# Attention kernel on one core: products with V on 64-row tiles in two banks, in two pieces a step

## The chip, the cores and the metric

The kernel runs on one core of one Trainium2 chip. The metric is device time in microseconds (us) of one execution. TensorE is PE in the profile (its weight loads PEld), VectorE is DVE, ScalarE is ACT, GpSimd is POOL, SyncE (which issues the DMAs) is SP.

## What is computed

A transformer block of 2048 tokens and width 512, all in float32: attention with 32 heads of 16 that share one key and one value head, then a gated feed-forward part of width 1792. Both are preceded by a layer norm that a vector c modulates.

```
mod = (silu(c) @ w_mod)          # sa, ca, ga, sb, cb, gb
h = layernorm(x) * (1 + ca) + sa
q = h @ wq  (32 heads of 16);  k = h @ wk;  v = h @ wv      # one k, one v
p = softmax(q k^T / 4);  o = p v
x = x + ga * (o @ wo)
h = layernorm(x) * (1 + cb) + sb
x = x + gb * ((sigmoid(h @ w_gate) * (h @ w_up)) @ w_down)
```

## The kernel before

**Units and steps.** The queries are cut into 4 blocks of 512 (b), the heads into 8 groups of four (u). A unit i is one (b, u); there are 32. Each unit has 16 steps, one for each 128 keys (kb), so there are 512 steps, s = 16 i + kb. After them comes a tail with the feed-forward part of the last block.

**A step.** `scores(n)` for n = 0 to 3 makes one tile of transposed scores `st` (128 keys x 512 queries, for one head; `st_tile`) and one tile `sa` of scores the other way round (128 queries x 512 keys; `a_tile`), which belongs to a later unit. ACT turns each `st` into exponentials `P`. DVE takes the row maxima of each `sa` (`mx`). The maxima go into spare rows of the queries `qp`, so that `st` comes out with the maximum already taken off. Queries and keys are split into high and low 16-bit halves that lie in one contraction of 64 rows, which is why `st` and `sa` have 64 rows: one takes the upper 64 rows of the array, the other the lower 64, and the two run at once.

**Products with V** (`pv`): for each of the four heads of the unit, V (128 keys x 32 columns, 16 of them ones, which give the softmax's sums) is the stationary operand and P the moving one, in float32. Head hh writes partitions 32 hh to 32 hh + 31 of one PSUM bank `c`, so a product takes 128 rows and 32 columns of the array, and four run at once. They lag the scores by LAG = 2 steps (`vq`). In a step with feed-forward work (`full`) all 512 queries are done in one piece, after `scores(1)`. In other steps they are done in two halves of 256, after `scores(1)` and after `scores(3)`. In unit 0 the order of keys and queries differs (`parts`), and a tile holds four pieces of 128 queries.

**The end of a unit** (`unit_end`): DVE copies `c` to `cs`; DMAs take the sums to DRAM (`lD`) and the rows to `raw`; some steps later (W1, W2, W3) the reciprocals come back and POOL multiplies.

**Maxima**: after the 64th `sa` tile of a unit, `max_end` reduces on DVE at the next step's start, and `max_rows` transposes the result on PE into a bank of the `sa` pool. ACT copies it out (`m`), POOL splits it, and DMAs put it into `qp`.

**Feed-forward work** of block b - 1 (and, in block 0, the remaining products for q) is laid between the scores of block b. A `Couple` holds two accumulation groups of 64-row products, so that two products run at once, each on one half of the array. `plan(s)` starts a couple, decides over how many steps it goes (RATE = 4.5 pairs a step) and lists the sizes of its places (`places`); `piece()` runs the next place. There are three places a step: after `scores(0)`, after `scores(2)` and after `scores(3)`. In the middle of a couple the two groups change halves, and one place there is left empty. The transposes of the normalised rows (`tr`, four for each group) go in two places of two. In block 0 `light(s)` places the q products after `scores(0)`.

**Order.** From the first step on, the order on PE, DVE and ACT is the order of the code (`keep`, by way of `Ordered`; hence line 116 for nearly all of it).

**PSUM** has 8 banks: `c` 1, `st` 2, `sa` 3, and 2 for everything else (`bank`).

Of the kernel before, what the change touches and what calls it, by code (L numbers as in the profile page):

```python
# [10 lines left out]
AF = mybir.ActivationFunctionType  # L11
ALU = mybir.AluOpType
# [10 lines left out]
QB = 512  # L23
NB = S // QB
NKB = S // P
NDC = D // P
NFC = F // P
NU = 8
# [14 lines left out]
LAG = 2  # L43
# [7 lines left out]
RATE = 4.5  # L51
# [6 lines left out]
W3 = 2  # L58

PBUFS = 4  # L60
SBANKS = {"st": 2, "sa": 3}
GWB = 3
HBUFS = 36

# [2 lines left out]
def adaln_mqa_glu_kernel(  # L67
# [15 lines left out]
    pool, sp = nc.gpsimd, nc.sync  # L83
# [16 lines left out]
    def bank(name):  # L100
        return psum["b"].tile([P, 512], F32, tag="b", name=name, bufs=psum.get("n", 7))

    def sbank(name):
        return psum["s"].tile([P, 512], F32, tag=name, name=name, bufs=SBANKS[name]) if "s" in psum else bank(name)

    def cbank(name):
        return pc.tile([P, 512], F32, tag="c", name=name, bufs=1)
# [10 lines left out]
    pinned = []  # L118
    pe, dve, act = Ordered(nc.tensor), Ordered(nc.vector), Ordered(nc.scalar)
# [45 lines left out]
    def t32(name, shape=(P, 512)):  # L165
        return wp.tile(list(shape), F32, tag="f32", name=name, bufs=18)
# [156 lines left out]
    V = cp.tile([P, NKB, 32], F32, name="V")  # L323
# [93 lines left out]
    Cs = {}  # L417
    Ps = {}
# [71 lines left out]
    def parts(i, t):  # L490
        if i == 0:
            return [(4 * (t % 4) + n, slice(n * P, (n + 1) * P), slice(t // 4 * P, (t // 4 + 1) * P)) for n in range(4)]
        return [(t, slice(0, QB), slice(0, QB))]
# [12 lines left out]

    def pv(i, t, half=None):
        if t == 0 and half != 1:  # L510
            Cs[i] = cbank("c")
        ps = parts(i, t)
        if half is not None:
            if i == 0:
                ps = ps[2 * half:2 * half + 2]
            else:
                cut = slice(half * QB // 2, (half + 1) * QB // 2)
                ps = [(t, cut, cut)]
        for kb, cols, qs in ps:
            for hh in range(4):  # L520
                pe.matmul(Cs[i][32 * hh:32 * hh + 32, qs], V[:, kb, :], Ps[i, t, hh][:, cols],
                          start=(kb == 0 and (i == 0 or half != 1)), stop=(kb == NKB - 1 and (i == 0 or half != 0)))
        if half == 0:
            return
        for hh in range(4):
            del Ps[i, t, hh]
        if t == NKB - 1:
            unit_end(i)

    def unit_end(i):  # L530
        b, u = units[i]
        o, v = u // 2, u % 2
        cs = t32("cs")
        if pinned:
            dve.tensor_copy(cs, Cs.pop(i))
        else:
            act.activation(cs, Cs.pop(i), AF.Identity)
        if v == 0:
            raws[b, o] = t32("raw")
        raw = raws[b, o]  # L540
        half = slice(4 * DH * v, 4 * DH * (v + 1))

        def rows(dst, r0):
            for hh in range(4):
                g = 4 * v + hh
                sp.dma_start(dst[DH * g:DH * (g + 1)], cs[32 * hh + r0:32 * hh + r0 + DH])

        if u >= NU - 2 and b == NB - 1:

            if v == 0:  # L550
                rbs[b, o] = t32("rb")
            rb = rbs[b, o]
            rows(rb, DH)
            rows(raw, 0)
            dve.reciprocal(rb[half], rb[half])
            if v == 0:
                return
        else:
            if v == 0:
                rbs[b, o] = dr.tile([2, 8, QB], F32, tag="lD", name="lD", bufs=2)  # L560
            lD = rbs[b, o]
            sp.dma_start(lD[0, 4 * v:4 * v + 4], cs[DH:P:2 * DH])
            rows(raw, 0)
            if v == 0:
                return
            defer(W1, lambda: recip(b, o, lD, raw))
            return
        finish(b, o, raw, rb, u == NU - 1 and b == NB - 1)

    def recip(b, o, lD, raw):  # L570
        lc = wp.tile([P, 32], F32, tag="lc", name="lc", bufs=2)
        rc = wp.tile([P, 32], F32, tag="rc", name="rc", bufs=2)
        sp.dma_start(lc, lD[0].rearrange("h (s e) -> (h s) e", e=32))
        defer(W2, lambda: recip2(b, o, lD, raw, lc, rc))
# [23 lines left out]
    def defer(n, f_):  # L598
        waits.append((now[0] + n, f_))
# [35 lines left out]
    class Transposes:  # L635
        stage, n = "tr", 4
# [196 lines left out]
    psum["s"] = psum["ctx"].enter_context(tc.tile_pool(name="pa", bufs=1, space=PSUM, reuse_waits="tile"))  # L833
    psum["b"], psum["n"] = psum["s"], 7 - sum(SBANKS.values())
    pinned.append(True)
# [16 lines left out]
    run = []  # L852
    lead = [0.0]
# [1 line left out]


    def places(m, n):
        skip = 3 * (n - n // 2) - 1
        res = [3 if k + 1 == skip else (1, 2, 1)[k % 3] for k in range(3 * n)]
        for ks in (range(skip), range(skip + 1, 3 * n)):  # L860
            order = sorted(ks, key=lambda k: ((0, 2, 1)[k % 3], k))
            while sum(res[k] for k in ks) != m:
                d = 1 if sum(res[k] for k in ks) < m else -1
                res[order[0]] += d
                order.append(order.pop(0))
        res[skip] = 0
        return res

    def pick(s):
        while main and main[0][0] is None:  # L870
# [15 lines left out]

    def plan(s):
        if s < NU * NKB:
            return None
        if not run:  # L890
            g = pick(s)
            if g is None:
                lead[0] = 0.0
                return None
            if g.stage == "tr":
                n, sizes = 1, [2, 0, 2]
            else:
                least = -(-g.n // MOST)
                n = min(max(least, round((g.n + lead[0]) / RATE)), len(units) * NKB - s)
                if n < least:  # L900
                    spare.insert(0, g)
                    return None
                sizes = places(g.n // 2, n)
            at = 0
            for k, z in enumerate(sizes):
                run.append((g, at, at + z, n if k == 0 else 0))
                at += z
        lead[0] += sum(z[2] - z[1] for z in run[:3]) - RATE
        return "run"

    def piece():
        if run:
            g, n0, n1, _ = run.pop(0)
            if n1 > n0:
                g.part(n0, n1)

# [5 lines left out]
            early[c_].part(ats[n], ats[n + 1])  # L922

    vq = []
    before = None

    for i, (b, u) in enumerate(units):
        if u == 0 and b > 0:
            wos, trs, gs = ffn_groups(b - 1)
            gs = [Couple(*wos[:2]), Couple(*wos[2:])] + trs + gs  # L930
            main.extend([(b - 1, g) for g in gs[:-KEPT]] + [(None, None)] + [(b - 1, g) for g in gs[-KEPT:]])
        for kb in range(NKB):
            s = i * NKB + kb
            now[0] = s
            late, pend[:] = pend[:], []
            for z in [z for z in waits if z[0] <= s]:
                waits.remove(z)
                z[1]()
            rows = [max_end(*z) for z in late]
            an = A0 + 4 * s  # L940

            def scores(n):
                st_tile(i, kb, n // 2, n % 2)
                if an + (n ^ 1) < len(alist):
                    a_tile(*alist[an + (n ^ 1)])

            scores(0)
            if before == "run":
                piece()
            elif b == 0:  # L950
                light(s)
            scores(1)
            now_ = plan(s)
            full = now_ is not None
            if len(vq) >= LAG:
                pv(*vq[0], None if full else 0)
            for z in rows:
                z()
            scores(2)
            if now_ == "run":  # L960
                piece()
            scores(3)
            if len(vq) >= LAG:
                if not full:
                    pv(*vq[0], 1)
                vq.pop(0)
            if now_ == "run":
                piece()
            before = now_
            vq.append((i, kb))  # L970
            while wdone < nw:
                if wdone < nw - 4 and (wdone + 0.5) * WSTEPS > (s + 1) * (nw - 4):
                    break
                if wdone >= nw - 4 and s < WLAST + 3 * (wdone - nw + 4):
                    break
                wjobs[wdone]()
                wdone += 1
# [1 line left out]
    while run:  # L979
        piece()  # L980
    while vq:
        pv(*vq.pop(0))
    assert not waits
    psum["ctx"].close()
    psum["ctx"] = ctx.enter_context(ExitStack())
# [44 lines left out]
```

## Time and profile before

| | |
|---|---|
| median of 3 runs | 1741.75 us (1739.81 to 1743.01) |
| span of the profiled execution | 1738.4 us |
| what lies around the span, to the median | 3.35 us |
| PE busy | 1691.9 us, 97% of the span |
| DVE busy | 1443.2 us, 83% |
| ACT busy | 1226.3 us, 71% |
| POOL busy | 605.1 us, 35% |
| mean granted TensorE clock | 0.983 |
| unit 0 (16 steps) | 115.4 to 158.6 us |
| units 1 to 7 (112 steps) | 158.6 to 451.3 us |
| tail | from 1592 us |

The page gives no time of the profiled execution apart from its span. A row of a group reads: line, engine, operation, written tile <- read tiles, shape, count | busy us, mean ns of one | idle us of the engine before them, and what ended it. For a matmul the shape begins with rows * columns of the array that it takes (64*128). A row of the timeline reads: start us, length us, engine, line, operation, tiles, shape, how many were merged. Matmuls are pipelined, so a record is longer than what it adds to the stream; starts tell more than lengths.

### The profile page before, as it was taken

The numbers are of one execution on the slowest core, as the hardware profiler recorded it, in microseconds if no ns is written. First come the engines' busy times: TensorE is split into PE (matmuls) and PEld (weight loads), VectorE is DVE, ScalarE is ACT, GpSimd is POOL, SyncE is SP. The second block draws the span as 40 slices with busy tenths as digits, with TensorE's granted clock in tenths as the row PEclk, the third lists the DMA queues.
The fourth block names the chain that finished last, engine by engine and source line by source line (L and its number), as shares of the span: only waits on it lengthen the run. The fifth ranks groups of instructions, "written<-read, shape, count | busy, mean of one in ns | idle before, by whom it ended". The sixth has DMA issues, their size and how long they took to land.

```text
span 1738.4 us, 35892 instructions
## 1 busy us (share of the span) xinstructions
PE 1691.9 (97%) x14467; PEld 591.1 (34%) x14467; DVE 1443.2 (83%) x2407; ACT 1226.3 (71%) x2231; POOL 605.1 (35%) x715
## 2 busy tenths in 40 slices
PE   5889999999999999999999999999999999999998
PEld 3335333333233333333333333333333333333443
DVE  8889999999998988888899898988898888841311
ACT  3338888888878777777778777777778777774100
POOL 4131445454443332332245232233255141231433
PEclk9769999999999999999999999999999999999999
DMA  7111223231100110111111110011101010011211
GB/s 262 40 47 31 95 85 106 89 110 63 51 23 26 47 49 12 33 38 41 32 41 33 33 50 20 26 47 47 36 17 57 28 57 5 30 50 55 75 60 49
DMA packets 66238, 90.94 MB, mean 52 GB/s; under 512 B 14752, under 2 KB 41376, under 8 KB 66072
## 3 DMA queue, kind: packets, MB, share of 16 engines
q1 hardware_dynamic: 66072, 88.66, 15.6%
q8 instruction: 113, 1.85, 0.4%
q14 instruction: 53, 0.43, 0.1%
HBM read 67.68 MB, written 16.22 MB: 48 GB/s over the span
## 4 chain that ended last, share of the span: by engine, by line
PE 86%; DVE 7%; ACT 2%; POOL 1%; issue 1%; DMA 1%; SPq 0%; POOLq 0%; DVEq 0%; ACTq 0%
PE c L116 27%; PE st L116 20%; PE pgu L116 12%; PE sa L116 8%; PE pd L116 5%; PE pgu L139 4%; DVE mx L116 3%; PE pd L139 2%; PE pq L116 2%; PE po L116 2%; ACT P L116 2%; PE sa L451 1%; DVE mx L453 1%; PE pmod L222 1%; PE pt L116 1%
## 5 line engine op out<-in xcount | busy, mean ns | idle before, releaser
L116 ACT ACTIVATE P<-st 128x512 f32<-128x512 f32 x2048 | 1139.2, 595 | 283.7 <-PE sa L116 250.0
L116 DVE TENSOR_REDUCE mx<-sa 128x1 f32<-128x512 f32 x1972 | 1241.2, 684 | 113.6 <-PE sa L116 108.3
L116 PE MATMUL st<-qp,kp 64*128 64x512 f16 (+1 forms) x2240 | 746.8, 362 | 7.1 <-DVE mx L453 2.4
L116 PE MATMUL sa<-kp,qp 64*128 64x512 f16 x1972 | 725.3, 382 | 0.5 <-DVE mx L116 0.5
L116 PE MATMUL c<-P,V 128*32 128x512 f32 (+2 forms) x5552 | 577.6, 492 | 2.9 <-DVE cs L116 2.9
L116 PEld LDWEIGHTS <-kp 64*128 64x128 f16 x2240 | 187.8, 94 | 500.1 <-issue 407.2
L116 PE MATMUL pgu<-h2h,gw 64*128 64x512 f16 x1344 | 242.6, 376 | 0.0
L116 PEld LDWEIGHTS <-qp 64*128 64x128 f16 x1972 | 181.8, 93 | 137.0 <-issue 51.9
L116 PEld LDWEIGHTS c<-P,V 128*32 128x32 f32 x5552 | 111.5, 108 | 192.1 <-issue 177.3
L727 POOL TENSOR_SCALAR th<-th 128x512 f32<-128x512 f32 x42 | 26.0, 619 | 335.8 <-ACT th L116 325.8
L116 PE MATMUL pgu<-h2l,gw 64*128 64x512 f16 x672 | 132.3, 376 | 0.0
L116 PEld LDWEIGHTS <-gw 64*128 64x128 f16 x2016 | 99.6, 94 | 80.7 <-issue 3.1
L424 POOL MEMSET qp<- 32x2048 f16 x32 | 57.6, 1798 | 49.3 <-PE st L116 41.6
L139 PE MATMUL pgu<-h2h,gw 128*128 128x512 f16 x224 | 66.8, 379 | 0.5 <-ACT h2h L283 0.5
L733 POOL TENSOR_TENSOR gl<-th,gh 128x512 f16<-128x512 f32 x56 | 64.8, 1157 | 4.7
L478 POOL TENSOR_SCALAR mh<-m 16x128 f16<-16x128 f32 (+1 forms) x34 | 9.8, 288 | 159.3 <-ACT m L116 159.0
L730 DVE SCALAR_TENSOR_TENSOR th<-th,pgu 128x512 f32<-128x512 f32 x14 | 9.6, 688 | 66.3 <-PE pgu L139 53.0
L248 POOL TENSOR_SCALAR wst<-wst 128x512 f32<-128x512 f32 x46 | 28.5, 620 | 102.1 <-DMA wst<-in_B_w_down_dram 27.1
L721 ACT ACTIVATE th<-pgu 128x512 f32<-128x512 f32 x14 | 8.4, 597 | 76.9 <-PE pgu L139 76.9
L116 DVE COPY u<-pgu 128x512 f32<-128x512 f32 x42 | 28.5, 679 | 35.7 <-PE st L116 19.8
L750 POOL TENSOR_TENSOR ot<-ot,gb 128x512 f32<-128x512 f32 x10 | 12.7, 1273 | 126.7 <-ACT ot L116 126.7
L590 POOL TENSOR_TENSOR raw<-raw,rb 128x512 f32<-128x512 f32 x15 | 19.1, 1273 | 102.7 <-DMA rb<-lD 84.1
(164 smaller groups left out, 1435.3 us busy)
## 6 DMA issues: line engine op xcount, KB each, us to landing
gw<-wD SPq DMA_DIRECT2D x56, 512.0 KB
wD<-gw SPq DMA_DIRECT2D x14, 512.0 KB
wm<-in_w_mod_dram SPq DMA_DIRECT2D x6, 1024.0 KB
qp<-qD SPq DMA_DIRECT2D x96, 64.0 KB
xall<-in_A_x_dram SPq DMA_DIRECT2D x4, 1024.0 KB
qD<-q SPq DMA_DIRECT2D x16, 256.0 KB
raw<-cs SPq DMA_DIRECT2D x128, 32.0 KB
xr<-in_A_x_dram SPq DMA_DIRECT2D x16, 256.0 KB
```

What stands on the lines that cost most here:

```text
L116: return (lambda *a, **k: keep(f_(*a, **k))) if pinned else f_
L139: pe.matmul(self.bank, l_, r_, start=(n == 0), stop=(n == self.n - 1))
L222: pe.matmul(p_[32 * k:32 * (k + 1)], cbc[:, k, :], wmods[i][:, k, :], start=True, stop=True)
L248: pool.tensor_scalar(w_, w_, SW, 0.0, op0=ALU.mult, op1=ALU.add)
L424: pool.memset(qp[j:j + 32], 0.0)
L451: pe.matmul(sa, qp[64 * j:64 * j + 64, pr0 + pr, qt * P:(qt + 1) * P], kp[64 * j:64 * j + 64, kc * 512:(kc + 1) * 512], start=True, stop=True)
L453: dve.tensor_reduce(mxs[i][:, 2 * j + pr, qt, kc:kc + 1], sa, axis=AX.X, op=ALU.max)
L478: pool.tensor_scalar(mh[:, 0], m32, 1.0, 0.0, op0=ALU.mult, op1=ALU.add)
L590: keep(pool.tensor_tensor(raw, raw, rb, op=ALU.mult))
L727: pool.tensor_scalar(th, th, 1.0, 1.0, op0=ALU.add, op1=ALU.mult)
L733: pool.tensor_tensor(lo, th, hi, op=ALU.subtract)
L750: pool.tensor_tensor(ot, ot, mods2['gb'], op=ALU.mult)
```

## The change

- **Products with V.** The contraction of 128 keys is cut into two of 64 (r = 0, 1). Each takes 64 rows and 32 columns of the array, so there are eight tiles. Row half 0 writes to bank `c`, row half 1 to a second bank `c1`. At a unit's end ACT copies the one bank, DVE the other, and POOL adds them (in the last unit DVE adds straight from PSUM).
- **Two pieces a step, always**: halves of 256 queries, normally after `scores(0)` and its feed-forward place, and after the third place. In the first step of a unit's products both are one turn later (`values`).
- **Banks.** `c1` takes one; `sa` has two instead of three.
- **Feed-forward work in four places a step**, one after each of the four scores; in the middle of a couple two places are empty. The transposes go in one place of four. `light(s)` and the maxima's transposes (`rows`) move one turn later.

```
-SBANKS = {"st": 2, "sa": 3}
+SBANKS = {"st": 2, "sa": 2, "c1": 1}
...
-    def pv(i, t, half=None):
-        if t == 0 and half != 1:
-            Cs[i] = cbank("c")
+    def pv(i, t, half):
+        if t == 0 and half == 0:
+            Cs[i] = (cbank("c"), sbank("c1"))
...
         for kb, cols, qs in ps:
-            for hh in range(4):
-                pe.matmul(Cs[i][32 * hh:32 * hh + 32, qs], V[:, kb, :], Ps[i, t, hh][:, cols],
-                          start=(kb == 0 and (i == 0 or half != 1)), stop=(kb == NKB - 1 and (i == 0 or half != 0)))
+            for r in range(2):
+                rs = slice(64 * r, 64 * r + 64)
+                for hh in range(4):
+                    pe.matmul(Cs[i][r][32 * hh:32 * hh + 32, qs], V[rs, kb, :], Ps[i, t, hh][rs, cols],
+                              start=(kb == 0 and (i == 0 or half == 0)),
+                              stop=(kb == NKB - 1 and (i == 0 or half == 1)))
...
-        cs = t32("cs")
-        if pinned:
-            dve.tensor_copy(cs, Cs.pop(i))
+        cs, cs1 = t32("cs"), t32("cs1")
+        c0, c1 = Cs.pop(i)
+        act.activation(cs, c0, AF.Identity)
+        if b == NB - 1 and u == NU - 1:
+            dve.tensor_tensor(cs, c1, cs, op=ALU.add)
         else:
-            act.activation(cs, Cs.pop(i), AF.Identity)
+            dve.tensor_copy(cs1, c1)
+            pool.tensor_tensor(cs, cs, cs1, op=ALU.add)
...
     def places(m, n):
...
+        k = 2 * n - 1
+        half = [m * (z + 1) // k - m * z // k for z in range(k)]
+        return half + [0, 0] + half
...
-                n, sizes = 1, [2, 0, 2]
+                n, sizes = 1, [0, 4, 0, 0]
...
+            plan(s)
+            vs = [(*vq[0], 0), (*vq[0], 1)] if len(vq) >= LAG else []
+            if vs and vs[0][1] == 0:
+                vs.insert(0, None)
+
+            def values():
+                if vs:
+                    z = vs.pop(0)
+                    if z is not None:
+                        pv(*z)
+
             scores(0)
-            if before == "run":
-                piece()
-            elif b == 0:
+            piece()
+            values()
+            scores(1)
+            if b == 0:
                 light(s)
-            scores(1)
-            now_ = plan(s)
-            full = now_ is not None
-            if len(vq) >= LAG:
-                pv(*vq[0], None if full else 0)
+            piece()
+            scores(2)
             for z in rows:
                 z()
-            scores(2)
-            if now_ == "run":
-                piece()
+            piece()
+            values()
             scores(3)
+            piece()
+            values()
             if len(vq) >= LAG:
-                if not full:
-                    pv(*vq[0], 1)
                 vq.pop(0)
-            if now_ == "run":
-                piece()
...
```

More of the change, by code (lines that the diff above doesn't have):

```diff
@@ L505, in st_tile @@
         Ps[i, t, 2 * pr + j] = p_[:, j]
-    def pv(i, t, half=None):
-        if t == 0 and half != 1:
-            Cs[i] = cbank("c")
+    def pv(i, t, half):
+        if t == 0 and half == 0:
+            Cs[i] = (cbank("c"), sbank("c1"))
         ps = parts(i, t)
[L513 to L518, printed above, removed]
-        for kb, cols, qs in ps:
-            for hh in range(4):
-                pe.matmul(Cs[i][32 * hh:32 * hh + 32, qs], V[:, kb, :], Ps[i, t, hh][:, cols],
-                          start=(kb == 0 and (i == 0 or half != 1)), stop=(kb == NKB - 1 and (i == 0 or half != 0)))
+        if i == 0:
+            ps = ps[2 * half:2 * half + 2]
+        else:
+            cut = slice(half * QB // 2, (half + 1) * QB // 2)
+            ps = [(t, cut, cut)]
+        for kb, cols, qs in ps:
+            for r in range(2):
[4 more added lines that the diff above has]
+                              stop=(kb == NKB - 1 and (i == 0 or half == 1)))
         if half == 0:
@@ L857, in places @@
     def places(m, n):
[L858 to L867, printed above, removed]
+        k = 2 * n - 1
+        half = [m * (z + 1) // k - m * z // k for z in range(k)]
+        return half + [0, 0] + half
     def pick(s):
@@ L888, in plan @@
         if s < NU * NKB:
-            return None
+            return
         if not run:
@@ L893, in plan @@
                 lead[0] = 0.0
-                return None
+                return
             if g.stage == "tr":
-                n, sizes = 1, [2, 0, 2]
+                n, sizes = 1, [0, 4, 0, 0]
             else:
@@ L901, in plan @@
                     spare.insert(0, g)
-                    return None
+                    return
                 sizes = places(g.n // 2, n)
             at = 0
-            for k, z in enumerate(sizes):
-                run.append((g, at, at + z, n if k == 0 else 0))
+            for z in sizes:
+                run.append((g, at, at + z))
                 at += z
-        lead[0] += sum(z[2] - z[1] for z in run[:3]) - RATE
-        return "run"
+        lead[0] += sum(z[2] - z[1] for z in run[:4]) - RATE
     def piece():
         if run:
-            g, n0, n1, _ = run.pop(0)
+            g, n0, n1 = run.pop(0)
             if n1 > n0:
@@ L924, in adaln_mqa_glu_kernel @@
     vq = []
-    before = None
     for i, (b, u) in enumerate(units):
@@ L945, in scores @@
                     a_tile(*alist[an + (n ^ 1)])
+            plan(s)
[7 more added lines that the diff above has]
+                        pv(*z)
             scores(0)
-            if before == "run":
-                piece()
-            elif b == 0:
+            piece()
+            values()
+            scores(1)
+            if b == 0:
                 light(s)
-            scores(1)
-            now_ = plan(s)
-            full = now_ is not None
-            if len(vq) >= LAG:
-                pv(*vq[0], None if full else 0)
+            piece()
+            scores(2)
             for z in rows:
                 z()
-            scores(2)
-            if now_ == "run":
-                piece()
+            piece()
+            values()
             scores(3)
+            piece()
+            values()
             if len(vq) >= LAG:
-                if not full:
-                    pv(*vq[0], 1)
                 vq.pop(0)
-            if now_ == "run":
-                piece()
-            before = now_
             vq.append((i, kb))
@@ L981, in adaln_mqa_glu_kernel @@
     while vq:
-        pv(*vq.pop(0))
+        for half in range(2):
+            pv(*vq[0], half)
+        vq.pop(0)
     assert not waits
```

## The prediction

> **What bounds the kernel now.** I read the page first, then busy time by stretch, the groups with shapes kept apart, and the timeline of single steps.
>
> ```profile
> span 1738.4 us, 35892 instructions
> PE 1691.9 (97%) x14467; PEld 591.1 (34%) x14467; DVE 1443.2 (83%) x2407; ACT 1226.3 (71%) x2231; POOL 605.1 (35%) x715
> PE 86%; DVE 7%; ACT 2%; POOL 1%; issue 1%; DMA 1%; SPq 0%; POOLq 0%; DVEq 0%; ACTq 0%
> ```
>
> PE carries 86% of the chain that ended last. A busy PE may still be slow inside, so I go by stretch (columns: PE, PEld, DVE, ACT, POOL busy us; clock; DMA).
>
> ```profile
> 158.60:451.30 292.70, 288.28 (x3032) 91.97 (x3028) 285.65 (x474) 252.97 (x463) 138.81 (x172) 1.00 0.27 87
> 540.80:1497.60 956.80, 955.86 (x7990) 315.84 (x7988) 859.43 (x1397) 744.64 (x1359) 306.10 (x347) 1.00 0.11 36
> ```
>
> The first row is units 1 to 7 of block 0 (112 steps): 292.7/112 = 2.61 us a step, PE and DVE both full. The second is 20 units with feed-forward work (320 steps): 2.99 us a step, PE at 99.9%, DVE at 90%. The granted clock is 1.00, so nothing comes from there.
>
> ```profile
> L116 PE MATMUL c<-P,V 128*32 128x512 f32 x2896 | 385.5, 604 | 0.0
> L116 PE MATMUL c<-P,V 128*32 128x256 f32 x2144 | 171.3, 391 | 2.9 <-DVE cs L116 2.9
> L116 PE MATMUL c<-P,V 128*32 128x128 f32 x512 | 21.1, 283 | 0.0
> ```
>
> Each product with V is two matmul records (two passes). A step with all 512 columns in one piece has 4 x 2 = 8 records: 2896/8 = 362 "whole" steps. A step in two halves has 16: 2144/16 = 134 "halved" steps. Unit 0 has 512/32 = 16. That is all 512 steps.
>
> **One whole step, one halved step.**
>
> ```profile
> 801.24 0.38 PE L116 MATMUL pgu<-h2h,gw 64*128 64x512 f16 x2
> 801.49 0.37 PE L116 MATMUL st<-qp,kp 64*128 64x512 f16 x1
> 801.50 0.39 PE L116 MATMUL sa<-kp,qp 64*128 64x512 f16 x1
> 801.82 1.06 PE L116 MATMUL c<-P,V 128*32 128x512 f32 x8
> 802.81 0.39 PE L116 MATMUL st<-qp,kp 64*128 64x512 f16 x1
> 802.82 0.39 PE L116 MATMUL sa<-kp,qp 64*128 64x512 f16 x1
> 803.04 0.38 PE L116 MATMUL pgu<-h2h,gw 64*128 64x512 f16 x2
> 803.26 0.38 PE L116 MATMUL sa<-kp,qp 64*128 64x512 f16 x1
> ...
> 351.08 0.64 PE L116 MATMUL c<-P,V 128*32 128x256 f32 x8
> 351.65 0.39 PE L116 MATMUL st<-qp,kp 64*128 64x512 f16 x1
> ```
>
> Two matmuls of 64 rows run side by side, one on each half of the array, and such a pair advances PE by 0.215 us (803.04 to 803.26). A piece of c lasts 0.99 us from its start to the next st for 512 columns (801.82 to 802.81) and 0.57 us for 256 (351.08 to 351.65). So 256 columns stream in 0.42 us, and 0.15 us of each piece does not depend on its width. Ahead of it, sa starts at 801.50, streams 0.215 us, and c starts 0.32 us after it: another 0.10 us. A piece therefore pays 0.25 us beyond its streaming, and PE's step adds up: 4 pairs of scores 0.86, feed-forward 4.5 pairs (RATE) 0.97, c 0.84 + 0.25 = 1.09; 2.92 of the 2.99 us.
>
> Is it the change of tile shape (the a*b in the rows) that costs the 0.25 us?
>
> ```profile
> 1591.63 0.61 PE L116 MATMUL c<-P,V 128*32 128x512 f32 x4
> 1592.17 0.39 PE L139 MATMUL po<-woh,ah 128*128 128x512 f16 x1
> ...
> 1620.46 0.38 PE L139 MATMUL pd<-wdh,gl 128*128 128x512 f16 x1
> 1620.67 0.49 PE L698 MATMUL pt<-ident,t 128*128 128x128 f32 x3
> ...
> 802.27 0.61 PE L116 MATMUL c<-P,V 128*32 128x512 f32 x4
> 802.29 0.59 PE L116 MATMUL c<-P,V 128*32 128x512 f32 x1
> ```
>
> At 1620.67 the type changes from f16 to f32 in one shape: 0.215 us after pd, no cost. At 1592.17 only the columns of the shape change (128*32 to 128*128, rows the same): the last second pass starts 0.02 us after the first of the four (802.27 and 802.29), so 1591.65 to 1592.17 is 0.52 us for 0.42 us of streaming, 0.10 us too long. That is just what c pays on its way to 64*128 (802.29 to 802.81, 0.52 us). A change of columns alone costs as much as a change of rows and columns.
>
> The Trainium skill ("TensorEngine Tiling (Array Packing)", section Key Properties) says that changing the tiling mode, and not just the tile, drains the TensorE, and its list of configurations has 64x128 and 64x32 as two modes. By that rule each new piece pays on entry and exit; the trace agrees where it can be seen, and no run here yet shows the two 64-row shapes side by side.
>
> **The change, part by part** (the sum is made against the span, 1738.4 us; the median of the runs, 1741.75, is 3.35 above it, and I add that at the end).
>
> (1) *Two pieces in every step.* The 362 whole steps pay for a second entry and exit: 362 x 0.25 = +90.5. If 64*32 beside 64*128 cost nothing, this would be a gain (rival B). I take the full 0.25 by the 1592.17 row, the nearest: a change of columns with equal rows. PE has no idle time there to hide it (955.86 of 956.80).
>
> (2) *Eight tiles instead of four.* The streaming stays 0.42 us per 256 columns if both halves of the array run together, as the st/sa pair does. Tiles start some 7 ns apart (0.02 us for three), so four more end the piece 0.027 us later: x 2 x 362 = +19.5; bounds 0 and twice that (39). The skill's "TensorE: Matmul & The Clock Gate" (Measured speedup vs the span model) has about 4 ns a tile, which would make this 11.6.
>
> (3) *Two banks for sa.* When does a bank come free?
>
> ```profile
> 1264.53 2.45 DVE L116 TENSOR_REDUCE mx<-sa 128x1 f32<-128x512 f32 x4
> 1265.24 0.37 PE L116 MATMUL sa<-kp,qp 64*128 64x512 f16 x1
> 805.70 0.39 PE L116 MATMUL sa<-kp,qp 64*128 64x512 f16 x1
> 806.15 2.48 DVE L116 TENSOR_REDUCE mx<-sa 128x1 f32<-128x512 f32 x4 [0.29 <-PE sa L116]
> PEld sa L116 <- DVE mx L116: 19.4, 25, 0.8
> L116 DVE TENSOR_REDUCE mx<-sa 128x1 f32<-128x512 f32 x1972 | 1241.2, 684 | 113.6 <-PE sa L116 108.3
> L116 DVE COPY u<-pgu 128x512 f32<-128x512 f32 x42 | 28.5, 679 | 35.7 <-PE st L116 19.8
> L116 DVE COPY cs<-c 128x512 f32<-128x512 f32 x32 | 22.0, 687 | 11.1 <-PE c L116 9.9
> L116 PE MATMUL sa<-ident,m 128*16 128x128 f32 x31 | 8.6, 277 | 0.5 <-DVE m L116 0.5
> ```
>
> A reduce starts 0.45 us after its matmul (805.70 to 806.15); reduces in a row come every 0.60 us ((2.45 - 0.68)/3, rounded); a waiting sa starts 0.71 us after its bank's reduce did (1264.53 to 1265.24). With three banks such waits sum to 19.4 us. With two, sa number k+2 waits for the start of reduce k plus 0.71, and st and all else on PE queue behind it. By hand:
> - Whole step, new order (pair 0.215, feed-forward 0.24 a place, piece 0.42 + 0.25 + 0.027 = 0.70): sa at 0, 1.155, 1.61, 2.77, next at 3.22; reduces start at 0.45, 1.60, 2.20, 3.22. The banks are wanted at 1.61, 2.77, 3.22 and free at 1.16, 2.31, 2.91: at least 0.3 us spare, no wait. Another DVE operation of 0.60 us can eat this and cost up to 0.3: 42 u copies and 24 cs1 copies (cs had them before), 66 x 0.3 = +20 (0 to 40).
> - Halved step (no feed-forward; the early q products, 24 pairs in 17 steps, 0.30): sa at 0, 0.915, 1.43, 2.345, PE ready again at 2.56; reduces at 0.45, 1.365, 1.965, 2.80; the next sa's bank is free only at 1.965 + 0.71 = 2.675. Carried on, it settles at 2.675 a step against 2.56 for PE alone, +0.115, and PE alone grows by 2 x 0.027: 0.17 x 112 = +19; the cs1 and q copies of 7 units 2 x 0.3 each, +4; unit 0 likewise 16 x 0.17 = +3; 22 halved steps later 0.05 each, +1. Sum +27 (6 with no bank waits, 45 if each copy costs its 0.60 and unit 0, with its 128-column products on eight tiles, 1 us a step).
>
> (4) *The maxima's transposes* (sa<-ident, 31). They move from behind c to behind sa in S2's place. There they pay an entry of their own, 31 x 0.10 = +3, and hold one of two banks until ACT has read it: in the hand schedule the bank is wanted at 1.83 and free at 1.60 + 0.71 = 2.31; half of that wait, 0.25 x 31 = +8 (0 to 15).
>
> (5) *Feed-forward in four places.* Pairs and their streaming are the same. The normalised rows' transposes go in one place instead of two:
>
> ```profile
> 527.14 0.39 PE L116 MATMUL sa<-kp,qp 64*128 64x512 f16 x1
> 527.46 0.44 PE L116 MATMUL pt<-ident,t 128*128 128x128 f32 x2
> 527.83 0.39 PE L116 MATMUL st<-qp,kp 64*128 64x512 f16 x1
> ```
>
> From sa to st 0.69 us, of which 0.215 + 2 x 0.11 stream: 0.25 us around such a place; one place less in 12 groups, -3.
>
> (6) *Adding the two banks of c.*
>
> ```profile
> L116 ACT ACTIVATE P<-st 128x512 f32<-128x512 f32 x2048 | 1139.2, 595 | 283.7 <-PE sa L116 250.0
> L590 POOL TENSOR_TENSOR raw<-raw,rb 128x512 f32<-128x512 f32 x15 | 19.1, 1273 | 102.7 <-DMA rb<-lD 84.1
> ```
>
> ACT copies c0 (0.60 us) and POOL adds (1.27 us, by its rows of the same shape), 32 times; ACT is at 71%, POOL at 35% and off the chain. If that cover were gone, 32 x 1.9 = 60 at most. Behind the ACT copy wait that step's exponentials. The next unit's first piece, which must find both banks empty, moves behind S2 and the second behind S3, some 1.9 us later: taken as 0. The stores of cs on SP leave about 2 us later, with two to three steps (6 to 9 us) planned for each hop. In the last unit an ACT copy and an add of 0.6 us each stand where one copy stood, hidden by the output products.
>
> Sum: 90.5 + 19.5 + 20 + 27 + 3 + 8 - 3 = +165; 1738.4 + 165 + 3.35 = 1907 us.
>
> **Rivals.** A is the forecast. Its ends: all small terms at their low bounds, 90.5 + 6 + 3 - 3 = +97, 1839; all high, 90.5 + 39 + 40 + 45 + 3 + 15 - 3 = +230, 1972.
>
> B, faster: 64-row shapes follow each other without the 0.10 us on each side. A piece then keeps only its first load and the tiles' starts, 0.05 + 0.027 = 0.077. Whole steps: 2 x 0.077 against 0.25, -0.096 x 362 = -35; with the starts hidden too, -35 - 2 x 0.047 x 362 = -69. The halved steps meet DVE's 4 x 0.60, say -0.05 x 112 = -6. Against it stand 20 + 3 + 8 - 3 = +28 from (3) to (5). Together -13 to -47, or +14 with (3) and (4) at their upper bounds: 1695 to 1756, middle 1715. With q for what a piece pays beyond its streaming, the balance is 362 x (2q - 0.25) + 28 - 6 = 0, so the change gains only where q is below 0.09 us. For B: the array is not regrouped by rows any more, and a pair of 64-row products does start within 0.01 us. Against: the 1592.17 row, where rows stayed too.
>
> C: the two row halves of the f32 products run one after the other: 0.84 us more in 512 steps, +430, 2170 and over. Against it stand the st/sa pairs; for it, only that no f32 product on 64 rows is shown.
>
> D: gains and losses cancel, 1738 to 1745.
>
> **How the numbers follow.** A 0.80, B 0.14, C 0.04, D 0.02. The measurement can tell 0.2% (3.5 us). Faster: B's 0.12. Same: 0.01 of B and 0.01 of D, 0.02. Slower: the rest, 0.86. The range for 8 in 10 is A's: up to 1965, just under its high end, and down to 1795, where each of the 724 pieces would pay 0.06 less than 0.25 with the small terms low as well. B, C and D lie outside, 0.20.
>
> **What would show it.** In whole steps: c in two groups of 16 records a step, each ending 0.10 us late before the next st, and a step near 3.3 us; in block 0 near 2.8 us. Waits of PEld sa for DVE mx well over 19.4 us. DVE's share in 540 to 1500 falls below 85%. Wrong if the last c record of a piece is followed by st after 0.42 us instead of 0.52 (B), if a piece streams 0.84 us (C), or if sa's waits stay near 20 us while the time still grows.

## The result, and the profile after

The changed kernel takes 1967.55 us (median of 4, 1967.14 to 1970.01) against 1742.34 us: ratio 1.1301, 95% interval 1.1284 to 1.1317. That is 225 us slower. The direction was forecast and the size was not: +165 us, with a range that ended at 1965.

The page of the kernel after: span, busy times, shares of the chain that ended last, and two groups.

```profile
span 1965.5 us, 58671 instructions
PE 1865.7 (95%) x25787; PEld 630.8 (32%) x25787; DVE 1471.8 (75%) x2407; ACT 1242.5 (63%) x2263; POOL 642.3 (33%) x744
PE 82%; DVE 6%; ACT 5%; issue 2%; DMA 2%; POOL 1%; SPq 1%; POOLq 0%; ACTq 0%; DVEq 0%
L116 DVE TENSOR_REDUCE mx<-sa 128x1 f32<-128x512 f32 x1972 | 1269.3, 685 | 291.3 <-PE sa L116 287.5
L116 PE MATMUL c<-P,V 64*32 64x256 f32 (+1 forms) x16896 | 680.1, 382 | 0.0
```

DVE now idles 291 us ahead of its reduces, waiting for PE, against 113.6 before. So PE is the bound still, and slower. The same stretches by units (columns as before; units 1 to 7, then 20 units with feed-forward work):

```profile
162.80:483.30 320.50, 313.67 (x4855) 95.38 (x4850) 292.79 (x473) 256.95 (x469) 147.22 (x178) 1.00 0.25 81
587.00:1701.50 1114.50, 1074.02 (x15566) 341.54 (x15564) 877.38 (x1395) 751.42 (x1378) 329.82 (x364) 1.00 0.10 31
```

A step takes 320.5/112 = 2.86 us in block 0 (2.61 before) and 1114.5/320 = 3.48 us later (2.99 before); 2.8 and 3.3 had been forecast. In the second stretch DVE is busy 79% of the time (877.38 of 1114.50), below the 85% that was to show the forecast. One piece of c, from PE's timeline:

```profile
901.16 0.38 PE L116 MATMUL pgu<-h2l,gw 64*128 64x512 f16 x2
901.47 0.66 PE L116 MATMUL c<-P,V 64*32 64x256 f32 x16
901.75 0.38 PE L116 MATMUL c<-P,V 64*32 64x256 f32 x2
902.06 0.39 PE L116 MATMUL st<-qp,kp 64*128 64x512 f16 x1
```

The feed-forward pair streams until 901.16 + 0.215 = 901.375 and c starts at 901.47: 0.10 us. The last records start at 901.75, stream 0.21 us, and st comes at 902.06: 0.10 us again. The piece lasts 0.59 us (901.47 to 902.06) against 0.57 of the old halves. The columns of the shape changed and the rows did not, and the price is the old one. Rival B is out, and C too.

Then a line that I had not forecast. The timeline at the end of a couple, all engines, after:

```profile
904.07 0.38 PE L116 MATMUL pgu<-h2h,gw 64*128 64x512 f16 x2
904.28 0.38 PE L116 MATMUL sa<-kp,qp 64*128 64x512 f16 x1
904.57 0.60 ACT L116 ACTIVATE th<-pgu 128x512 f32<-128x512 f32 x1
904.69 0.68 DVE L116 COPY u<-pgu 128x512 f32<-128x512 f32 x1
905.22 0.58 PE L116 MATMUL pd<-wdh,gh 64*128 64x512 f16 x2 [0.55 <-ACT th L116]
```

and the same place before (its PE rows stand in the prediction: last pair 801.24, c 801.82 to 802.81, next couple 803.04):

```profile
801.93 0.59 ACT L116 ACTIVATE th<-pgu 128x512 f32<-128x512 f32 x1
802.20 0.68 DVE L116 COPY u<-pgu 128x512 f32<-128x512 f32 x1
```

The pool for everything else has two banks, and a couple takes both; ACT's th and DVE's u empty them. Before, ACT and DVE emptied them under a pair of scores, the whole piece of c and another pair, 1.8 us. After, the next couple's first place comes one pair of scores later, and PE waits: from sa at 904.28, plus 0.215 of streaming, to 905.22 are 0.72 us. The view of waits, after:

```profile
PEld sa L116 <- DVE mx L116: 28.0, 31, 1.7
PE pgu L116 <- ACT th L116: 18.0, 31, 0.8
PE sa L116 <- DVE mx L116: 16.2, 39, 1.3
```

Each row gives who waited for whom, us in total, how often, and the longest. The waits of PEld sa grew from 19.4 to 28.0 us, and those of PE sa, 0.8 us before, to 16.2: the sign that the prediction named. For the couples the view shows too little. It counts idle time from the modelled end of the record ahead, 0.17 us after its streaming ended, so it shows 0.55 where 0.72 was lost. Counted by starts in the trace, 43 first products of a couple come late in the 320 steps, by 31 us in sum.

### The profile page after: what moved, and what is told of

It reads as the page before. It is cut to its first block, busy times and chain, and to the rows that moved or that the text cites. A ratio compares the mean times of both kernels' runs of the same rounds, so it can differ in the third digit from the quotient of the medians.

```text
span 1965.5 us, 58671 instructions
## 1 busy us (share of the span) xinstructions
PE 1865.7 (95%) x25787; PEld 630.8 (32%) x25787; DVE 1471.8 (75%) x2407; ACT 1242.5 (63%) x2263; POOL 642.3 (33%) x744
## 4 chain that ended last, share of the span: by engine, by line
PE 82%; DVE 6%; ACT 5%; issue 2%; DMA 2%; POOL 1%; SPq 1%; POOLq 0%; ACTq 0%; DVEq 0%
PE c L116 28%; PE st L116 19%; PE pgu L116 10%; PE sa L116 9%; PE pd L116 4%; PE pgu L139 4%; DVE mx L116 3%; PE pd L139 2%; ACT P L116 2%; PE pq L116 2%; PE po L116 1%; ACT th L116 1%; PE sa L451 1%; DVE mx L453 1%; SPq L551 1%
## 5 line engine op out<-in xcount | busy, mean ns | idle before, releaser
L116 DVE TENSOR_REDUCE mx<-sa 128x1 f32<-128x512 f32 x1972 | 1269.3, 685 | 291.3 <-PE sa L116 287.5
L116 PE MATMUL c<-P,V 64*32 64x256 f32 (+1 forms) x16896 | 680.1, 382 | 0.0
L116 PEld LDWEIGHTS c<-P,V 64*32 64x32 f32 x16896 | 193.5, 105 | 425.4 <-issue 407.4
L116 PE MATMUL pgu<-h2h,gw 64*128 64x512 f16 x1312 | 258.2, 377 | 26.2 <-ACT th L116 18.0
L116 PEld LDWEIGHTS <-qp 64*128 64x128 f16 x1972 | 175.5, 93 | 108.0 <-issue 32.1
L542 POOL TENSOR_TENSOR cs<-cs,cs 128x512 f32<-128x512 f32 x31 | 39.3, 1268 | 181.6 <-DVE cs L116 169.3
L139 PE MATMUL pgu<-h2h,gw 128*128 128x512 f16 x240 | 71.9, 379 | 0.0
L116 PE MATMUL pd<-wdh,gh 64*128 64x512 f16 x280 | 56.4, 376 | 4.9 <-ACT ot L116 2.6
L737 POOL TENSOR_SCALAR gh<-th 128x512 f16<-128x512 f32 x56 | 34.8, 621 | 69.1 <-DVE th L735 65.5
```

The costliest lines, as they stand in the source:

```text
L116: return (lambda *a, **k: keep(f_(*a, **k))) if pinned else f_
L139: pe.matmul(self.bank, l_, r_, start=(n == 0), stop=(n == self.n - 1))
L542: pool.tensor_tensor(cs, cs, cs1, op=ALU.add)
L737: pool.tensor_scalar(hi, th, 1.0, 0.0, op0=ALU.mult, op1=ALU.add)
```

## The experiments

Each kernel's median stands with the kernel before at 1740.6 to 1742.7 us on the same chip.

**b_two: a second piece alone.** In the kernel before:

```
-            full = now_ is not None
+            full = False
```

> The kernel before, with the products with V in two halves of 256 queries in the 362 whole steps too (128 rows, one bank, three banks for sa). Theory M: a second entry and exit of 0.25 us in 362 steps, +90, 1832 us; somewhat less, down to 1815, if the shorter pieces take away stalls of the scores. Rival B' (what a piece pays is not the change of shape but the wait of the next scores for their banks, which shorter pieces ease): below 1780 us.

1827.2 us, +86 (1.0492, 1.0476 to 1.0507). Term (1) of the forecast, 90.5, is shown, and rival B' falls.

**b_sa2: two banks for sa alone.** In the kernel before:

```
-SBANKS = {"st": 2, "sa": 3}
+SBANKS = {"st": 2, "sa": 2, "c1": 1}
```

> The kernel before with two banks for sa; the bank that comes free lies idle. Theory M: by the hand schedule +0.115 us in 112 halved steps, +13, and 0 to 20 us in the whole steps, the transposes of maxima +8: 1755 to 1785 us. Rival S (the two banks are most of what the forecast missed): 1800 us or more.

1833.1 us, +92 (1.0530, 1.0514 to 1.0546). My expectation was wrong and rival S's number was met: in the order before the bank is worth as much as a second piece. The 20 units by stretch in b_sa2, then DVE's wait in the kernel before and in b_sa2:

```profile
572.30:1587.60 1015.30, 1013.04 (x7991) 326.49 (x7988) 862.42 (x1397) 752.27 (x1359) 306.40 (x347) 1.00 0.11 34
```

```profile
DVE mx L116 <- PE sa L116: 108.3, 280, 0.9
```

```profile
DVE mx L116 <- PE sa L116: 184.9, 394, 1.3
```

Before, the same stretch had 7990 matmuls and 955.86 us busy of 956.80; here it has 7991 and 1013.04 of 1015.30. PE is 99.9% and 99.8% busy, with equal work, 58 us apart: short waits vanish in the busy time, since records are longer than what they stream. DVE's idle time shows them, and so do the starts. In these 320 steps sa starts more than 0.03 us behind its st in 455 places, by 74 us in sum; before it was 23 places and 3 us. Of the 74 us, 67 lie at the third and fourth scores after a piece of c. A bank comes free 0.45 + 0.71 = 1.16 us after its sa started, at the earliest (by the rows under (3) of the prediction). With two banks the third sa needs the bank of the first, and in the step shown for the kernel before the third st comes 1.09 us after the first (802.81; 803.90 in a row under a_near). My hand schedule had been drawn for the new order alone, where a piece of c between them puts the third 1.61 us after the first.

**b_64rows: eight tiles, the rest as b_sa2.** The products, the second bank and the end of a unit are those of the kernel after; pieces, places and order are those of the kernel before.

> The kernel before with the products with V on eight tiles of 64 rows and 32 columns in two banks, c added at the end of a unit as in the kernel after, two banks for sa; pieces, places and their order as before. Theory M: against the kernel before with two banks for sa 0.027 us more a piece, 362 + 2 x 134 pieces, +17 us (0 to 30). Rival T (the shape of 64 rows is itself slow, in its loads or its issue): more than 60 us over the kernel before with two banks for sa. Rival B (the change between shapes of 64 rows costs less): 100 us or more below that kernel.

1846.1 us (1.0596, 1.0578 to 1.0614): 13 us over b_sa2, where 17 were expected. Rivals B and T fall. These 13 us also hold what the copies and the addition at a unit's end cost.

**a_128, a_128_sa3, a_128_b3: the order after, with the old products.** In the kernel after, `pv` runs over heads alone, on 128 rows, and `unit_end` copies the one bank as before. The freed bank lies idle, goes to sa, or goes to the pool of the rest:

```
 SBANKS = {"st": 2, "sa": 2, "c1": 1}     # a_128
 SBANKS = {"st": 2, "sa": 3}              # a_128_sa3
 SBANKS = {"st": 2, "sa": 2}              # a_128_b3
```

> The kernel after with the products with V back on four tiles of 128 rows and 32 columns in one bank, copied out as before; the second bank of c lies idle, so sa keeps two; two pieces a step, four places, all as after. Theory M (eight tiles cost 0.027 us a piece and the change between shapes of 64 rows costs as much as the old one): 1024 pieces x 0.02 to 0.027, 20 to 28 us less than after, 1940 to 1948 us. Rival B (64-row shapes change more cheaply): slower than after, 1990 us or more. Rival T (the 64-row shape itself is slow): below 1900 us.

1943.2 us (1.1160, 1.1142 to 1.1179), 24 less than after: eight tiles cost 24 us.

> As the run with 128 rows in the order after, with the idle bank given back to sa, so three. Theory M: PE's blocks of scores and feed-forward work stand still 36 us more in 320 steps than before (without the couples' waits), and 25 us more in block 0; both go: 55 to 70 us below the run with two banks, 1875 to 1890 us. Rival S' (the bank costs what it costs in the order before, 92 us): 1850 us or less. Rival by the forecast (20 + 8 + 23 us, half of it here): 1915 us.

1880.2 us (1.0791, 1.0775 to 1.0807), 63 less than a_128. So sa's third bank is worth 63 us in this order: by the starts of the units 24 us of it in units 1 to 7, and 38 later. In the 20 units it is 30 us, and there the sa that start more than 0.03 us behind their st go from 32 us in sum to 3.

> As the run with 128 rows in the order after, with the idle bank given to the pool of everything else, so that pool has three and sa keeps two. Theory M (a couple's first product waits for banks that ACT and DVE empty): one of the two groups no longer waits, the other still may; 10 to 31 us below the run with 128 rows and two. Rival S (PE is held by sa, the couples' waits only stand in for it): within 5 us.

1926.2 us (1.1065, 1.1048 to 1.1083), 17 less than a_128. The first of a couple's products no longer waits. The second does, 21 us in the 320 steps by the starts in the trace.

**a_gap and a_sa3_gap: a couple's first place left empty**, in the kernel after and in a_128_sa3:

```
-        return half + [0, 0] + half
+        k -= 1
+        return [0] + [m * (z + 1) // k - m * z // k for z in range(k)] + [0, 0] + half
```

> The kernel after, with a couple's first place left empty, so that its first product comes one pair of scores and one piece of c later; all else, the number of places too, as after. Theory M (the gap between forecast and result is the couples' banks: PE waits 0.73 us at 43 starts of a couple in 320 steps, 31.2 us, until ACT and DVE have emptied the couple before): 31 to 37 us less than after, 1930 to 1937 us. Rival S (the two banks of sa hold PE up, and these waits would come back elsewhere): within 8 us of 1967.

1947.8 us (1.1182, 1.1165 to 1.1199), 20 less than after, where 31 to 37 were expected. The couples' waits are gone from the trace, but the sa that start more than 0.03 us behind their st go from 28 us in 153 places to 45 us in 193: with two banks for sa a part comes back. Neither theory M nor rival S had the number.

> The run with 128 rows, three banks for sa and the order after, with a couple's first place left empty. Theory M (what the order after adds over two pieces in the order before, 1880 against 1827 us, is mainly the couples' first products waiting 0.73 us for banks, 43 times in 320 steps): 25 to 35 us less, 1845 to 1855 us. Rival O (the order of scores and pieces itself, with a place behind each pair of scores): within 8 us of 1880.

1841.5 us (1.0565, 1.0546 to 1.0584), 39 less than a_128_sa3. With three banks for sa the whole of it is got, 33 us of it in the 20 units, and rival O is left with 14 us over b_two. Only 3 of these 14 us lie in the 20 units; the rest is spread over the other stretches, with 4 behind the last score. In the views of waits of a_128_sa3 and a_sa3_gap, the first has this line and the second has none of its kind:

```profile
PE pgu L116 <- ACT th L116: 17.8, 31, 0.8
```

**a_one: one piece a step in the kernel after.** Both halves come behind the third feed-forward place.

```
-            vs = [(*vq[0], 0), (*vq[0], 1)] if len(vq) >= LAG else []
+            vs = [None, [(*vq[0], 0), (*vq[0], 1)]] if len(vq) >= LAG else []
```

> The kernel after with both pieces of a step in one place, behind the third feed-forward place, so one change of shape each way a step instead of two. By the price of the shapes alone: 0.26 us x 496 steps, 129 us less than after, 1838 us. Theory M (the long piece starves DVE where sa has two banks, as it did in the order before with two banks, 0.2 us a step against 0.11): 40 to 75 us of it come back, 1880 to 1915 us. Rival B (no price of the shapes): 1967 us or more.

2053.8 us (1.1792, 1.1774 to 1.1810): 86 slower than after, and 139 above the top of what was expected. Halving the changes of shape lost more than it saved. The timeline of a_one around one piece:

```profile
1001.63 1.28 DVE L116 TENSOR_REDUCE mx<-sa 128x1 f32<-128x512 f32 x2
1002.28 1.09 PE L116 MATMUL c<-P,V 64*32 64x256 f32 x32
1003.31 0.39 PE L116 MATMUL sa<-kp,qp 64*128 64x512 f16 x1
1003.73 1.08 ACT L116 ACTIVATE P<-st 128x512 f32<-128x512 f32 x2 [1.13 <-PE sa L116]
1003.77 1.29 DVE L116 TENSOR_REDUCE mx<-sa 128x1 f32<-128x512 f32 x2 [0.86 <-PE sa L116]
```

DVE and ACT run dry under the long piece (0.86 and 1.13 us idle). Then PE, with four scores to do before the next piece, waits for their banks. The group of st's products on the pages of after and a_one ends with the idle time ahead of them and what ended it:

```profile
L116 PE MATMUL st<-qp,kp 64*128 64x512 f16 (+1 forms) x2240 | 748.6, 364 | 15.0 <-ACT P L116 10.6
```

```profile
L116 PE MATMUL st<-qp,kp 64*128 64x512 f16 (+1 forms) x2240 | 738.2, 361 | 101.7 <-ACT P L116 93.3
```

**b_one: one piece in block 0 of the kernel before.**

```
-            full = now_ is not None
+            full = now_ is not None or (b == 0 and i > 0)
```

> The kernel before with one piece in block 0's units 1 to 7 as well (112 steps, three banks for sa). By the price of the shapes alone: 0.25 us x 112 = 28 us less, 1713 us. Theory M (a long piece starves DVE and ACT where little feed-forward work lies between the scores, also with three banks): these steps get longer, by 0 to 0.35 us, 1741 to 1782 us.

1780.2 us, +38 (1.0213, 1.0199 to 1.0228). Units 1 to 7 in b_one:

```profile
158.60:490.00 331.40, 279.01 (x2164) 78.94 (x2162) 288.22 (x473) 249.80 (x462) 138.29 (x171) 1.00 0.24 77
```

They took 292.7 us before, and PE now has 52 us of open idle time. On the page of b_one PE's st wait 53.4 us for ACT's P (2.0 us in the view of waits before): the third bank of sa does not help the two of st. Fewer changes of shape are no gain where little lies between the scores.

```profile
L116 PE MATMUL st<-qp,kp 64*128 64x512 f16 (+1 forms) x2240 | 744.6, 361 | 58.0 <-ACT P L116 53.4
```

**a_near: a_sa3_gap with one piece in the steps with feed-forward work**, behind the second place:

```
+            whole = run and vs
+            if whole:
+                vs = []
...
             piece()
+            if whole:
+                pv(*vq[0], 0)
+                pv(*vq[0], 1)
             scores(2)
```

> The run with 128 rows, three banks for sa and the empty first place, with both halves of c in one place behind the second feed-forward place in steps that have feed-forward work: what is left of the change is four places against three. Theory M (a second piece costs 0.25 us a step and, with three banks, one piece does not starve DVE in these steps): 75 to 90 us below 1842, 1750 to 1767 us. Theory M', by the run that put the kernel after into one piece and lost 86 us (a long piece starves DVE in this order too): 1842 us or more.

1859.8 us (1.0688, 1.0671 to 1.0706): 18 more than a_sa3_gap, so M fell. M' had the number, but its reason, that DVE starves, is not all of it: st's banks hold PE up too. A step behind the piece in a_near, PE and then ACT:

```profile
1002.31 0.39 PE L116 MATMUL st<-qp,kp 64*128 64x512 f16 x1
1002.53 0.38 PE L116 MATMUL pgu<-h2l,gw 64*128 64x512 f16 x2
1002.75 0.38 PE L116 MATMUL st<-qp,kp 64*128 64x512 f16 x1
1002.97 0.38 PE L116 MATMUL pgu<-h2h,gw 64*128 64x512 f16 x2
1003.38 0.37 PE L116 MATMUL st<-qp,kp 64*128 64x512 f16 x1
```

```profile
1002.73 2.32 ACT L116 ACTIVATE P<-st 128x512 f32<-128x512 f32 x4 [1.17 <-PE sa L116]
```

PE has streamed its pair by 1003.18, and the third st starts 0.2 us later, 0.65 us after ACT began on the first at 1002.73: it had waited for one of two st banks. In the order before, one, two and one pairs lie between the scores that follow c, and the fourth score is followed by c at once. So there the third st came 1.09 us after the first (802.81 in the prediction) and had its bank; the row before:

```profile
803.90 0.38 PE L116 MATMUL st<-qp,kp 64*128 64x512 f16 x1
```

Four even places put less behind c and keep one for ahead of it. In the 320 steps late st behind feed-forward products sum to 41 us here and 5 us before. This is read from the traces; no run tried the old sizes in this order.

**b_tr: the transposes beside c** in the kernel before, all four in one place right behind the piece:

```
-                n, sizes = 1, [2, 0, 2]
+                n, sizes = 1, [4, 0, 0, 0]
...
+            if run and run[0][0].stage == "tr" and run[0][1] == 0 and run[0][2] == 4:
+                piece()
             scores(2)
```

> The kernel before with the four transposes of a group in one place, right behind the piece of c, so that going to their shape and back costs one 0.10 us instead of two places of 0.25 us. By the price of the shapes: 12 groups x 0.35 to 0.4 us, 4 to 5 us less, 1737 us. Rival: PE's block without scores grows from 1.1 to 1.6 us in 12 steps and DVE or ACT run dry: no gain.

1750.4 us, +8 (1.0046, 1.0031 to 1.0060). All of the difference lies in the units that hold transposes (unit 9: 3.06 us a step against 2.87; units 18, 25 and 26 likewise). The rival held, and one of these steps in the trace shows how: behind the piece and the transposes ACT has idled 1.06 us and DVE 1.12 us, ACT first reads the transposes out (532.17, 0.78 us), and PE then stands 0.86 us ahead of a st (533.48) that waits for ACT's exponentials. No version tried here beats the kernel before.

## Why the prediction was wrong, by its own steps

The measured runs make a chain from one kernel to the other:

| step | run | us | gain or loss | forecast |
|---|---|---|---|---|
| kernel before | | 1741 | | |
| second piece | b_two | 1827 | +86 | (1) 90.5 |
| order and places after, first place empty | a_sa3_gap | 1842 | +14 | (4) 3 and (5) -3 |
| couples start at once | a_128_sa3 | 1880 | +39 | none |
| two banks for sa | a_128 | 1943 | +63 | (3) 20 + 27, (4) 8 |
| eight tiles, two banks of c | after | 1968 | +24 | (2) 19.5, (6) 0 |

The shares depend on the order of the steps. Taken out of the kernel after itself, the couples' wait is worth 20 us (a_gap) and not 39, and the two banks for sa then come, by difference, to 82 us and not 63 if the eight tiles cost the same 24 there, which no run shows.

- **(1) and (2) held.** The price is per change of shape, rows or columns, 0.10 us each way; the row at 1592.17 was the right one to go by. b_64rows puts 13 us on 630 pieces on eight tiles, and a_128 24 us on 1024: 0.021 and 0.024 us a piece where 0.027 had been taken.
- **(3) and (4) came near in sum** in this chain, 63 against 55 (which counts 6 us of tile starts in block 0): 24 us in units 1 to 7, where the hand schedule gave 19 + 4; 38 later, where it gave 20 + 8. There is luck in it: by the difference above the same bank is worth 82 us once the couples' waits are gone, and it is worth 92 us in the order before (b_sa2).
- **(5) is the step that failed.** "Pairs and their streaming are the same" priced the work and not the time between two couples. Forecast 0 with the transposes' entry, measured +53 in the chain: 39 for couples that start one pair of scores after the last one ended, which a_sa3_gap shows, and 14 for the rest of the new order, whose cause stays open. The old order hid the emptying of two banks under c and two pairs of scores, 1.8 us; I looked for a wait that the change adds at c and at sa only, and not at the third pool of banks, whose count did not change. The kernel after without this wait, a_gap, takes 1947.8 us, inside the range.
- **(6) was not measured alone.** No line of the view of waits has PE waiting for the new copies, and in the order before it is at most a part of the 13 us of b_64rows.
- **Rivals.** B and C are refuted by the 901.47 rows, by b_64rows and by a_128, D by the result. (The balance of rival B comes to q = 0.095 us and not 0.09, which changes nothing here.) The range left 58 us above the middle; the 53 of (5) and the 8 of (3) and (4) took up all of it and, with the smaller misses, 2.5 us more.

## What to carry to other kernels

Moving work to more places leaves its sum as it was and changes the distance between the last use of a bank and its next; price that distance for every pool of banks, also for those whose size stays. A change of tile shape has its price each time, but fewer and longer pieces pay only while the scores that then come closer together do not wait for banks: here a second piece cost 86 us in one order, and going back to one lost 86 and 18 us in another. Where a matmul's record is longer than what it streams, look for short waits in the starts and in the idle time of the engines behind, not in PE's busy share.

## What the runs showed of the hardware

- Going from 64*128 to 64*32 and back costs 0.10 us each way (901.375 to 901.47; 901.96 to 902.06), as from 128*32 to 64*128 or to 128*128: equal rows bring nothing.
- Eight float32 products on 64*32 tiles run together: 256 columns of all eight in 0.59 us with entry load and exit, against 0.57 us for four on 128*32. Their starts lie 7 ns apart.
- A third bank for one stream of tiles was worth 63 us in one order and 92 us in another, with PE busy over 99% in the stretch of b_sa2 that lost 58 of them.
